# Attention and a routed expert layer on one core: weight, token and quarter sums moved from GpSimd to VectorE, slot lists by column ops, and new ranks

## The chip, the core and the metric

The kernel runs on one core of a Trainium2 chip. The core has TensorE (PE in the profile; PEld is its weight load), VectorE (DVE), ScalarE (ACT), GpSimd (POOL), SyncE (SP), which issues transfers, and 16 DMA engines. Each engine runs its own list of instructions in order and waits on semaphores for the others. The metric is the device time of one execution in microseconds; lower is better.

## The reference, cut to what matters

Eight sequences of 576 tokens with eight heads of 64 go through attention over a window of 128 tokens with a bias that grows with distance. The result, 4608 rows of 512, goes through a layer of eight experts of which each token takes two.

```python
scores = scale * q @ k.T + bias           # only 0 <= i - j < 128 counts
x = softmax(scores) @ v                   # heads side by side: [4608, 512]

noisy = x @ w_gate + log1p(exp(x @ w_noise)) * noise
top2 = two largest of noisy per token     # of 8 experts
top2_w = softmax over those two
for e in range(8):
    h = maximum(x[mask] @ w1[e], 0)       # 512 -> 1024
    out[mask] += top2_w * (h @ w2[e])     # 1024 -> 512
```

## The kernel before

**Order of the work.** The program is written as strands (Python generators). A strand yields an `Op` with an engine, a cost in microseconds and a rank, or an `Event`, or a ring of buffers. While the kernel is built, the class `Order` plays the strands through a simulated clock: each engine takes the waiting Op of least rank, and the instructions are emitted in that order. So every engine's list is fixed at build time by the costs and by the ranks, which come from constants at the top of the file (`LOAD`, `GATE`, `ROUTE`, `SCATTER`, `STAGE`, `LATE`, `SIZES` and so on). `either` offers an Op to ScalarE and VectorE, and `added` offers it to VectorE and GpSimd; whichever is free first by the simulated clock takes it, with one of the numbers of `LATE` as a handicap.

**Attention.** 32 head pairs are loaded, multiplied (`scores`), biased and reduced on VectorE (`top`, L540 and L548), exponentiated on ScalarE (`soft`, L564), transposed, masked on GpSimd (`split`, L597 and L598), and multiplied with the values (`weigh`). Rows go to DRAM (`xs`), and `gate` makes the logits of the experts.

**Routing.** For each sequence b, `route(b)` finds the two experts of each token (MAX8 at L852), gives each of the 2 x 5 choices per partition a slot number, and splits that into a line `ln` and a place `pl`. Then `which` (L891) compares all ten places with the numbers 0 to 63 in one instruction, and all ten lines with 0 to 79 in another, and `numbered` (L896) multiplies the first of these one-hots by the token numbers, on GpSimd or, in the last sequence, on VectorE. Ten products on TensorE (`list_`, L900) make the list of tokens by slot, which GpSimd adds into DRAM.

**Experts.** Expert 0 starts early in three blocks while the attention ends. The other seven have two blocks of 512 tokens (`wide`) and a smaller one each. All inputs are split into two half-precision parts (hi and lo), so a product takes three passes. A wide block's first layer works on halves: the 512 x 512 product of each pair of weight chunks is made from seven products of quarters (a scheme of Strassen's kind) and needs sums of quarters on three sides:

- weights, `summed_weights`: four subtractions of 128x256 in two parts (L1134) for each of 28 chunk pairs, then a cast `hi` and a residue `lo` (L1149);
- tokens, `turn_pair`: four adds or subtractions (L1337, L1338, L1340, L1341) for each of 28 pairs of token tiles, then a cast and residues (L1357), then a DMA transpose;
- products, `up_wide`: copies of the first two quarters (`copied`), their sum with two others in one op of 512 columns (`two_sums`, L1507), one more add of 256 columns behind it (L1510), sums with PSUM (`last_sum`, L1516), ReLU (L1546 on ScalarE, L1548 on VectorE) and residues (L1524, L1535). `two_sums` releases TensorE's next product, L1447.

`scaled_weight` casts the weights themselves (L279 on ScalarE or L281 on VectorE) and makes their residues (L1285). The second layer (L1578 for wide blocks, L1583 and L1571 for others) accumulates in PSUM; `result` scales by the gates and GpSimd adds the rows into the output by an indirect DMA (L1682). Gathers of token rows are L1295, also on GpSimd.

The sums are offered to both engines, in the token case as follows:

```python
    def added(a, b, rank, late, emit):
        return Op((("DVE", a, rank + max(late, 0.0)), ("POOL", b, rank + max(-late, 0.0))), lambda e: emit(engine[e]))
...
        for part in range(2):
            yield added(ADD * 2, ADDP * 2, rank, LATE[13], lambda g, part=part: sums_(g, part))
```

Of the kernel before, what the change touches and what calls it, by code (L numbers as in the profile page):

```python
# [8 lines left out]
F32 = mybir.dt.float32  # L9
F16 = mybir.dt.float16  # L10
BF16 = mybir.dt.bfloat16
I32 = mybir.dt.int32
U32 = mybir.dt.uint32
AF = mybir.ActivationFunctionType
OP = mybir.AluOpType
# [3 lines left out]
B, H, S, D = 8, 8, 576, 64  # L19
N, DM, E, F = B * S, H * D, 8, 1024  # L20
W = 128
NQ = 5
# [10 lines left out]
LINE, SPAN = 64, 10  # L33
# [6 lines left out]
WIDE, HALF = 512, 256  # L40
REST = CAP - 2 * WIDE
BLOCKS = tuple(((FROWS, c - FROWS),) if z < NF else ((0, WIDE), (WIDE, WIDE), (2 * WIDE, c - 2 * WIDE)) for z, c in enumerate(CAPS))
ZERO, EMPTY = -360.1, -14
LOAD = -70.1
VALUES = 211.5
GATE = (-6.6, 90.4, 356.8, 1.5)
ROUTE = (2.7, 19.6, 30.3, 85.8)
SCATTER = (192.6, -636.6, -1198.2, -775.2, -416.9)
FFN0, FFN1 = 160.9, 226.9
WEIGHTS = (150.4, 304.8)  # L50
TOKENS = 300.4
STAGE = (-13.0, 20.0, 8.1, -75.6, -10.3, 716.5, 87.3, 19.0)
MIDDLE = 77.8
RESULT = -175.8
SIZES = (35.1, -207.3, 1265.1)
SOON = -114.2
TIGHT = (1, 5, 7)
QUICK = (5, 7)
LATE = (-38.8, -263.4, 73.0, 226.7, -304.2, -361.8, -81.1, -258.9, 76.0, 16.9, -38.5, -10.3, -151.5, -115.4, 75.0)
LAG = 0.2  # L60
ADD, ADDP, TWS = 0.36, 0.9, 5
BEHIND = 2.7
TURN, MARGIN, LATE_BY = (0.3, 0.3), 1.0, 1.0
TURNED = 7e4
SLACK = 0.8
PACE, READ_BY, AHEAD = 0, 2.0, -28.3
HELD = 3
SWITCH, NEAR = 0.093, 3.6
TOP, SOFT, SPLIT = (1.27, 1.52, 0.92), (1.56, 1.56, 0.8), (0.85, 1.35, 0.85)
SP_COST = 0.45  # L70
DMA_RATE = 300e3
# [31 lines left out]
class Order:  # L103
# [15 lines left out]
    def spawn(self, strand):  # L119
        self.alive += 1  # L120
        self.at(self.now, lambda: self.advance(strand, None))
# [115 lines left out]
def attention_moe(ctx: ExitStack, tc: tile.TileContext, qk_, v, w_gate, w_noise, noise, w1, w2,  # L237
                  out, xs, slots, eye):
    nc = tc.nc
# [12 lines left out]
    spawn, put, mark = order.spawn, order.put, order.set  # L252
# [10 lines left out]
    def dve(us, rank, emit, join=True):  # L263
        return Op((("DVE", us, rank),), emit, join)
# [3 lines left out]

    def either(a, b, rank, late, emit):
        return Op((("ACT", a, rank), ("DVE", b, rank + late)), emit)  # L270

    engine = {"DVE": nc.vector, "POOL": nc.gpsimd}

    def added(a, b, rank, late, emit):
        return Op((("DVE", a, rank + max(late, 0.0)), ("POOL", b, rank + max(-late, 0.0))), lambda e: emit(engine[e]))

    def copy(e, o, i, **kw):
        if e == "ACT":
# [49 lines left out]
    steps_ = const.tile([128, E * SPAN], F16, name="steps")  # L328
# [489 lines left out]
    def route_tiles(z):  # L818
        return [ap_.tile(shape, dt, name=f"{name}{z}") for name, shape, dt in (
            ("y", [128, NQ, E], F32), ("u", [128, NQ, E], F32), ("l", [128, NQ, E], F32), ("tp", [128, NQ, 8], F32),  # L820
            ("idx", [128, NQ, 8], U32), ("ef", [128, NQ, 2], F32), ("oh", [128, NQ, 2, E], F32), ("both", [128, NQ, E], BF16),
            ("d", [128, NQ, 2], F32), ("gg", [128, NQ, 2], F32), ("rk", [128, NQ, E], F32), ("oh2", [128, NQ, 2, E], F32),
            ("ln", [128, NQ, 2], I32), ("pl", [128, NQ, 2], I32), ("gd", [128, NQ, E], F32), ("listed", [E * SPAN, LINE], F32),
            ("hot80", [128, 2 * NQ, E * SPAN], F16), ("hot64", [128, 2 * NQ, LINE], F16))]

    route_sets = [route_tiles(z) for z in range(2)]
# [2 lines left out]
    def route(b):  # L829
        yield gates[b]  # L830
        if b > 1:
            yield routed[b - 2]
        y_, u, l, tp, idx, ef, oh, both_, d, gg, rk, oh2, ln, pl, gd, listed, *hot = route_sets[b % 2]
        rank = 20 * b - ROUTE[kind(b)]
        V = nc.vector
        on, G, us = (dve, V, 0.75) if b == B - 1 else (pool, nc.gpsimd, 1.5)
        on_, N_ = (dve, V) if b in QUICK else (pool, nc.gpsimd)
        lg = lgs[b % 2]
        yield act(0.09, rank, lambda: nc.scalar.activation(u, lg[:, :, 8:16], AF.Abs))
# [45 lines left out]
        def lines_and_places():  # L885
            V.tensor_scalar(ln, pl, 6, None, op0=OP.arith_shift_right)
            V.tensor_scalar(pl, pl, LINE - 1, None, op0=OP.bitwise_and)

        def which(n_, of, hot_):
            shape = [128, 2 * NQ, n_]  # L890
            V.tensor_tensor(hot_, of.rearrange("p i k -> p (i k)")[:, :, None].to_broadcast(shape),  # L891
                            steps_[:, None, 0:n_].to_broadcast(shape), op=OP.is_equal)

        def numbered():
            t = hot[1].rearrange("p (i k) c -> p i (k c)", k=2)
            G.tensor_tensor(t, t, numbers[:, :, None].to_broadcast([128, NQ, 2 * LINE]), op=OP.mult)  # L896

        def list_(a):
            for z in range(2 * NQ):
# [60 lines left out]
        yield from chain(place, 0.3)  # L960

        mark(placed_)
        yield dve(0.75, rank, lambda: which(LINE, pl, hot[1]))
        spawn(number_them(on, us, rank, numbered, ready := Event()))
        yield dve(1.12, rank, lambda: which(E * SPAN, ln, hot[0]))
        yield ready
        a = yield (tb, rank)
        yield pe(0.4, rank, lambda: list_(a))
        yield dve(0.3, rank, lambda: whole_numbers(a))
# [16 lines left out]
    def first_ids(blk, cut, rank):  # L986
# [17 lines left out]
        blk.ix, blk.at = ix, cl  # L1004
        mark(blk.ids)
        spawn(weights_back(blk, rank))

    def number_them(on, us, rank, numbered, ready):
        yield on(us, rank, numbered)
        mark(ready)  # L1010

    def gates_out(b, rank, tp, d, oh, gg, gd, placed_):

# [111 lines left out]
    def summed_weights(e, a, rank, low, high):  # L1125

        (r0, there0, uses0), (r1, there1, uses1) = low, high
        done, (hi, lo) = sums[e, a]
        yield there0
        yield there1  # L1130
        s_ = yield (tsr, rank)

        def sums_(g, part):
            sub = lambda o, x, y: g.tensor_tensor(s_[:, 2 * o:2 * o + 2], x, y, op=OP.subtract)  # L1134
            if part == 0:
                sub(0, r1[:, 0:2], r0[:, 0:2])
                sub(2, r1[:, 2:4], r1[:, 0:2])
            else:
                sub(1, r1[:, 2:4], s_[:, 0:2])
                sub(3, r0[:, 2:4], s_[:, 2:4])  # L1140

        for part in range(2):
            yield added(ADD * 2, ADDP * 2, rank, LATE[12], lambda g, part=part: sums_(g, part))
        through_with(raw1, r0, uses0)
        through_with(raw1, r1, uses1)
        yield sized[e]
        sc = wsc[:, e, 0:1].bitcast(F32)
        yield either(1.04, 0.66, rank, LATE[5], lambda g: copy(g, hi, s_, scale=sc))
        yield dve(1.2, rank, lambda: nc.vector.scalar_tensor_tensor(lo, s_, sc, hi, op0=OP.mult, op1=OP.subtract))  # L1149
        put(tsr, s_)  # L1150
        yield order.now + SLACK
        mark(done)
# [162 lines left out]
    def turn_pair(blk, q, xp, rank):  # L1315
# [28 lines left out]
        nothing_ = hi[:, 0:4 * HALF].rearrange("p (a b) -> p a b", a=2)  # L1344
        yield act(1.12, rank, lambda: nc.scalar.activation(nothing_, rows, AF.Square, accum_out=big))
        for part in range(2):
            yield added(ADD * 2, ADDP * 2, rank, LATE[13], lambda g, part=part: sums_(g, part))
        yield dve(1.0, rank, powers)
        extra = xp[:, 2 * P:2 * P + 3 * HALF]
        parts_ = ((slice(0, 4 * HALF), rows, 4), (slice(4 * HALF, 7 * HALF), extra, 3))  # L1350
# [151 lines left out]
    def two_sums(c, y, rank, end, copies, done, u):  # L1502
        yield end
        for copy_ in copies:
            yield copy_
        both = c[:, 0:2].rearrange("p a b -> p (a b)")
        yield dve(0.6, rank - MIDDLE, lambda: nc.vector.tensor_tensor(both, y, both, op=OP.add))  # L1507
        yield order.now + SLACK
        mark(done)
        yield added(ADD, ADDP, rank - MIDDLE, LATE[14], lambda e: e.tensor_tensor(c[:, 4], c[:, 0], c[:, 1], op=OP.add))  # L1510
        mark(u)

    def last_sum(c, at, t, rank, end, ready_, done, whole):
# [478 lines left out]
```

## Time and profile before

| | |
|---|---|
| median of 3 runs | 1052.37 us (1047.01 to 1054.67) |
| profiled execution: time, span | 1055.15 us, 1053.4 us |
| busy, PE / DVE / ACT / POOL | 976.6 / 843.3 / 555.6 / 512.2 us |
| share of the span | 93% / 80% / 53% / 49% |
| mean granted clock of TensorE | 0.979 |

The span runs from the first to the last instruction. Busy time is the union of an engine's instructions. Matmuls are pipelined, so a busy TensorE is not one at its peak; in the attention stage its products are short. A wait is put down to the op that released it last.

### The profile page before, as it was taken

The page shows a single profiled execution, that of the slowest core. Times are in us where ns is not written, and L with a number is a line of the kernel's source. Part 1 is how long each engine was busy: PE and PEld are TensorE (multiplying, and loading weights), DVE is VectorE, ACT ScalarE, POOL GpSimd, SP SyncE. Part 2 cuts the span into 40 slices and gives each one's busy share as a digit, 9 for nine tenths or more (in the row PEclk, how much of TensorE's full clock was granted, in tenths as well). Part 3 has the DMA queues.
Part 4 walks back from the last instruction along what each step waited for, and adds up shares of the span by engine and source line. Part 5 has one row for each costly group of instructions (what it writes and reads, how often), then busy time and mean ns, then how long its engine had stood idle before and what let it go on. Part 6 is the DMA issues. An engine that isn't in the chain of part 4 may idle for free. (4 is left out here: it accounts for less than half of the span.)

```text
span 1053.4 us, 24584 instructions
## 1 busy us (share of the span) xinstructions
PE 976.6 (93%) x8656; PEld 669.9 (64%) x8656; DVE 843.3 (80%) x2639; ACT 555.6 (53%) x1484; POOL 512.2 (49%) x726
## 2 busy tenths in 40 slices
PE   8999998989998699979998999999899979998996
PEld 5766666655567466756676667666766666566663
DVE  8989999997668979696979898769978787879430
ACT  8988888832244445454543554445546354445221
POOL 3457677574444643633463437353726264553312
PEclk9999999989999999999999999999999989998998
DMA  9867897734699879777977679677979686776123
GB/s 324 310 212 251 271 344 236 274 68 108 139 221 203 193 214 161 173 156 205 134 155 171 178 144 181 171 205 167 143 220 194 167 194 157 143 166 114 29 29 49
DMA packets 236334, 188.84 MB, mean 179 GB/s; under 512 B 147056, under 2 KB 190352, under 8 KB 236208
## 3 DMA queue, kind: packets, MB, share of 16 engines
q1 hardware_dynamic: 218864, 148.31, 53.3%
q0 software_dynamic: 17344, 38.94, 20.2%
q8 instruction: 68, 1.11, 0.4%
q14 instruction: 58, 0.48, 0.1%
HBM read 116.24 MB, written 40.71 MB: 149 GB/s over the span
## 5 line engine op out<-in xcount | busy, mean ns | idle before, releaser
L1682 POOL DMA_INDIRECT out_dram<-yo,ix x69 | 114.6, 1662 | 72.4 <-ACT yo L279 30.0
L1578 PEld LDWEIGHTS <-hh 128*128 128x128 f16 x896 | 88.1, 99 | 84.3 <-issue 2.7
L1546 ACT ACTIVATE hh<-bank 128x256 f16<-128x256 f32 (+8 forms) x125 | 44.2, 356 | 142.7 <-PE bank L1421 82.0
L1447 PEld LDWEIGHTS <-wth 128*128 128x128 f16 x896 | 88.7, 99 | 37.9 <-issue 18.0
L1578 PE MATMUL bank<-w2ha,hl 128*128 128x512 f16 x288 | 110.1, 382 | 0.7 <-DVE hl L1535 0.7
L1578 PE MATMUL bank<-w2ha,hh 128*128 128x512 f16 x288 | 110.4, 383 | 0.0
L1578 PE MATMUL bank<-w2la,hh 128*128 128x512 f16 x288 | 110.2, 383 | 0.0
L1546 ACT ACTIVATE hh<-c 128x256 f16<-128x256 f32 (+1 forms) x98 | 50.2, 521 | 111.0 <-DVE c L1516 90.6
L564 ACT ACTIVATE p<-p,nm 128x128 f32<-128x128 f32 x256 | 99.3, 398 | 1.7 <-DVE nm L540 1.6
L1510 POOL TENSOR_TENSOR c<-c 128x256 f32<-128x256 f32 x32 | 32.3, 1010 | 125.6 <-DVE c L1507 106.7
L1578 PEld LDWEIGHTS <-hl 128*128 128x128 f16 x448 | 44.2, 99 | 55.0 <-issue 1.9
L279 ACT ACTIVATE c<-bank 128x256 f32<-128x256 f32 x92 | 34.3, 382 | 83.6 <-PE bank L1447 82.6
L1295 POOL DMA_INDIRECT xg<-xs_dram,ix x34 | 36.5, 1074 | 85.6 <-DVE ix L1042 55.3
L1447 PE MATMUL bank<-xhw,wth 128*128 128x256 f16 x224 | 62.9, 281 | 15.8 <-DVE c L1507 14.9
L1507 DVE TENSOR_TENSOR c<-bank,c 128x512 f32<-128x512 f32 x56 | 38.3, 684 | 47.0 <-PE bank L1447 46.4
L597 POOL TENSOR_SCALAR_AFFINE_SELECT pT<-pT 128x256 f32<-128x256 f32 (+1 forms) x80 | 45.5, 569 | 62.5 <-ACT pT L279 58.7
L540 DVE CUSTOM_DVE_ANT_0 p<-bank,bias 128x128 f32<-128x128 f32 x288 | 66.9, 283 | 0.9 <-ACT raw L1251 0.3
L1561 DVE SCALAR_TENSOR_TENSOR hl<-bank,hh 128x384 f16<-128x384 f32 (+8 forms) x88 | 31.1, 362 | 42.9 <-ACT hh L1546 38.5
L1447 PE MATMUL bank<-xhw,wtl 128*128 128x256 f16 x224 | 63.1, 281 | 0.8 <-DVE wtl L1149 0.8
L1447 PE MATMUL bank<-xlw,wth 128*128 128x256 f16 x224 | 63.1, 282 | 0.0
L1578 PE MATMUL bank<-w2hb,hh 128*128 128x512 f16 x160 | 61.1, 382 | 0.0
L1447 PE MATMUL bank<-xhe,wth 128*128 128x256 f16 x224 | 61.1, 273 | 0.0
(351 smaller groups left out, 3327.8 us busy)
## 6 DMA issues: line engine op xcount, KB each, us to landing
raw<-in_w_dram SPq DMA_DIRECT2D x144, 256.0 KB
mraw<-in_w_dram SPq DMA_DIRECT2D x56, 512.0 KB
qk<-in_qk_dram SPq DMA_DIRECT2D x32, 576.0 KB
vraw<-in_v_dram SPq DMA_DIRECT2D x16, 640.0 KB
out_dram<-xg SPq DMA_DIRECT2D x10, 1024.0 KB
xs_dram<-x SPq DMA_DIRECT2D x32, 256.0 KB
out_dram<-yo,ix POOLq DMA_INDIRECT x69
xs_dram<-x SPq DMA_DIRECT2D x8, 128.0 KB
```

The costliest lines, as they stand in the source:

```text
L279: nc.scalar.activation(o, i, AF.Copy, **kw)
L540: nc.vector.tensor_tensor_reduce(out=o, in0=i, in1=by, scale=-0.125, scalar=3.0e38, op0=OP.add, op1=OP.min, accum_out=m)
L564: nc.scalar.activation(pv, pv, AF.Exp, bias=nm[:, z, h:h + 1], scale=-1.0, accum_out=den[:, i, 2 * g + h:2 * g + h + 1])
L597: nc.gpsimd.affine_select(b, a, pattern, OP.is_ge, nothing, base=0, channel_multiplier=-1)
L1295: nc.gpsimd.indirect_dma_start(out=o, out_offset=None, in_=xs[0:blk.rows], in_offset=bass.IndirectOffsetOnAxis(ap=blk.at[0:r, j:j + 1], ax ...
L1447: nc.tensor.matmul(t, wp[:, at + kc], xp[:, 2 * o + kc], start=not add and kc + z == 0, stop=kc + z == 3, skip_group_check=add)
L1507: yield dve(0.6, rank - MIDDLE, lambda: nc.vector.tensor_tensor(both, y, both, op=OP.add))
L1510: yield added(ADD, ADDP, rank - MIDDLE, LATE[14], lambda e: e.tensor_tensor(c[:, 4], c[:, 0], c[:, 1], op=OP.add))
L1546: nc.scalar.activation(o, i, AF.Relu)
L1561: yield dve(0.07 + c * 0.00104, rank - MIDDLE, lambda: nc.vector.scalar_tensor_tensor(hl[:, 0:c], t[:, 0:c], 0.0, hh[:, 0:c], op0=OP.max, ...
L1578: nc.tensor.matmul(blk.y[j], h[:, cs], wp, start=a == 0 and z + m == 0, stop=a == 3 and z + m == 3)
L1682: ins = nc.gpsimd.indirect_dma_start(out=out, out_offset=bass.IndirectOffsetOnAxis(ap=blk.ix[0:r, j:j + 1], axis=0), in_=t[0:r], in_offset ...
```

## The change

All three kinds of sums are put on VectorE alone; `added`, the table of engines and the price of an add on GpSimd are gone, and the price of one on VectorE is 0.34 instead of 0.36. In the routing, line and place numbers are copied to floating point (`at`); instead of two wide compares and a multiplication there are twenty ops on VectorE, each of which makes one one-hot from a row of numbers and a scalar of its partition: ten of 64 columns that compare and multiply by the token number in the same op, and ten of 80 columns that compare. The strand that did the multiplication (`number_them`) is gone. All the constants that set ranks, handicaps and the lead of loads have other values.

```diff
-ZERO, EMPTY = -360.1, -14
-LOAD = -70.1
-VALUES = 211.5
-GATE = (-6.6, 90.4, 356.8, 1.5)
-ROUTE = (2.7, 19.6, 30.3, 85.8)
-SCATTER = (192.6, -636.6, -1198.2, -775.2, -416.9)
-FFN0, FFN1 = 160.9, 226.9
-WEIGHTS = (150.4, 304.8)
-TOKENS = 300.4
-STAGE = (-13.0, 20.0, 8.1, -75.6, -10.3, 716.5, 87.3, 19.0)
-MIDDLE = 77.8
-RESULT = -175.8
-SIZES = (35.1, -207.3, 1265.1)
-SOON = -114.2
+ZERO, EMPTY = -369.7, -14
+LOAD = -176.0
+VALUES = 264.2
+GATE = (28.7, 58.3, 273.1, -24.4)
+ROUTE = (-6.5, -64.7, 50.7, 56.9)
+SCATTER = (52.9, -732.8, -1277.6, -718.6, -208.6)
+FFN0, FFN1 = 159.2, 160.4
+WEIGHTS = (260.2, 307.4)
+TOKENS = 130.0
+STAGE = (128.3, 25.5, 7.9, -55.5, -24.4, 650.6, 199.2, 2.0)
+MIDDLE = 37.7
+RESULT = -108.3
+SIZES = (37.8, -49.2, 1152.7)
+SOON = -196.5
...
-LATE = (-38.8, -263.4, 73.0, 226.7, -304.2, -361.8, -81.1, -258.9, 76.0, 16.9, -38.5, -10.3, -151.5, -115.4, 75.0)
+LATE = (-36.7, -187.9, 194.5, 187.3, -443.9, -321.4, -78.2, -270.0, 39.8, 18.4, 65.3, -170.3, -195.9, -63.5, 40.7)
-ADD, ADDP, TWS = 0.36, 0.9, 5
-BEHIND = 2.7
+ADD, TWS = 0.34, 5
+BEHIND = 2.3
-PACE, READ_BY, AHEAD = 0, 2.0, -28.3
+PACE, READ_BY, AHEAD = 0, 2.0, 12.9
-SWITCH, NEAR = 0.093, 3.6
+SWITCH, NEAR = 0.093, 7.0
...
-            ("ln", [128, NQ, 2], I32), ("pl", [128, NQ, 2], I32), ("gd", [128, NQ, E], F32), ("listed", [E * SPAN, LINE], F32),
+            ("lp", [128, 2, NQ, 2], I32), ("at", [128, 2, NQ, 2], F32), ("gd", [128, NQ, E], F32), ("listed", [E * SPAN, LINE], F32),
...
             V.tensor_scalar(pl, pl, LINE - 1, None, op0=OP.bitwise_and)
-
-        def which(n_, of, hot_):
-            shape = [128, 2 * NQ, n_]
-            V.tensor_tensor(hot_, of.rearrange("p i k -> p (i k)")[:, :, None].to_broadcast(shape),
-                            steps_[:, None, 0:n_].to_broadcast(shape), op=OP.is_equal)
-
-        def numbered():
-            t = hot[1].rearrange("p (i k) c -> p i (k c)", k=2)
-            G.tensor_tensor(t, t, numbers[:, :, None].to_broadcast([128, NQ, 2 * LINE]), op=OP.mult)
+            V.tensor_copy(at, lp)
+
+        def places():
+            for z in range(2 * NQ):
+                i, k = z // 2, z % 2
+                V.tensor_scalar(hot[1][:, z], steps_[:, 0:LINE], at[:, 1, i, k:k + 1], numbers[:, i:i + 1],
+                                op0=OP.is_equal, op1=OP.mult)
+
+        def lines():
+            for z in range(2 * NQ):
+                V.tensor_scalar(hot[0][:, z], steps_[:, 0:E * SPAN], at[:, 0, z // 2, z % 2:z % 2 + 1], None, op0=OP.is_equal)
...
-        yield dve(0.75, rank, lambda: which(LINE, pl, hot[1]))
-        spawn(number_them(on, us, rank, numbered, ready := Event()))
-        yield dve(1.12, rank, lambda: which(E * SPAN, ln, hot[0]))
-        yield ready
+        yield dve(0.7, rank, places)
+        yield dve(0.7, rank, lines)
...
-            yield added(ADD * 2, ADDP * 2, rank, LATE[12], lambda g, part=part: sums_(g, part))
+            yield dve(ADD * 2, rank, lambda part=part: sums_(nc.vector, part))
...
-            yield added(ADD * 2, ADDP * 2, rank, LATE[13], lambda g, part=part: sums_(g, part))
+            yield dve(ADD * 2, rank, lambda part=part: sums_(nc.vector, part))
...
-        yield added(ADD, ADDP, rank - MIDDLE, LATE[14], lambda e: e.tensor_tensor(c[:, 4], c[:, 0], c[:, 1], op=OP.add))
+        yield dve(ADD, rank - MIDDLE, lambda: nc.vector.tensor_tensor(c[:, 4], c[:, 0], c[:, 1], op=OP.add))
```

## Rows read from the trace of the kernel before

**Rows 1.** Table of stages: stretch and length, busy us of PE, PEld, DVE, ACT, POOL, PEclk, DMA, GB/s.
```profile
0.00:240.00 240.00, 220.12 (x2895) 151.09 (x2896) 222.79 (x1152) 192.01 (x778) 147.80 (x318) 0.98 0.75 251
340.00:1000.00 660.00, 617.45 (x4720) 429.72 (x4720) 537.01 (x1211) 317.64 (x610) 307.02 (x334) 0.98 0.76 166
```

**Rows 2.** Waits of TensorE, 340 to 1000 us: total us, times, longest us.
```profile
PE bank L1447 <- DVE c L1507: 14.9, 6, 5.2
PE bank L1583 <- DVE hl L1561: 6.4, 7, 2.1
...
PE bank L1663 <- DVE yt L283: 0.2, 1, 0.2
```

**Rows 3.** Sums on GpSimd: stages of L1134 (DVE, POOL busy); groups by line, 240:1053.4.
```profile
340.00:1000.00 660.00, 16.03 (x34) 67.96 (x74) 0.98 0.76 166
...
L1510 POOL TENSOR_TENSOR c<-c 128x256 f32<-128x256 f32 x32 | 32.3, 1010 | 125.6 <-DVE c L1507 106.7 <-DVE wex L506 10.5 <-DVE diag L493 5.0
...
L1337 POOL TENSOR_TENSOR xp<-xp 128x256 f32<-128x256 f32 x8 | 10.8, 1346 | 3.2 <-ACT hh L1546 2.8 <-ACT w2ha L279 0.4
...
L1337 POOL TENSOR_TENSOR xg<-xg 128x256 f32<-128x256 f32 x4 | 4.2, 1046 | 0.1
```

**Rows 4.** Single lines: ns at minimum, median and maximum, first and last start, shapes.
```profile
L1516 DVE TENSOR_TENSOR c<-bank,c x112: 401/414/426, 350.0 to 1025.0; 128x256 f32<-128x256 f32 x112
...
L1285 DVE SCALAR_TENSOR_TENSOR w2lb<-raw,wsc,w2hb x20: 733/742/1207, 334.1 to 972.5; 128x512 f16<-128x512 f32 x20
...
L1535 DVE SCALAR_TENSOR_TENSOR hl<-c,hh x56: 672/682/1218, 352.9 to 1025.3; 128x512 f16<-128x512 f32 x56
...
L1524 DVE SCALAR_TENSOR_TENSOR hl<-c,hh x56: 406/418/1180, 351.8 to 1025.9; 128x256 f16<-128x256 f32 x56
...
L281 DVE TENSOR_SCALAR w1ha<-raw,wsc x14: 474/480/943, 81.6 to 955.2; 128x512 f16<-128x512 f32 x14
...
L1357 DVE SCALAR_TENSOR_TENSOR th<-xp,fit,th x28: 996/1274/1856, 324.4 to 968.5; 128x1024 f16<-128x1024 f32 x14, 128x768 f16<-128x768 f32 x14
...
L1510 POOL TENSOR_TENSOR c<-c x32: 717/728/1721, 348.7 to 1022.6; 128x256 f32<-128x256 f32 x32
L1510 DVE TENSOR_TENSOR c<-c x24: 406/416/978, 384.0 to 1003.9; 128x256 f32<-128x256 f32 x24
```

**Rows 5.** Groups of VectorE by line and shape, 240:1053.4: busy us, mean ns, idle before.
```profile
L1535 DVE SCALAR_TENSOR_TENSOR hl<-c,hh 128x512 f16<-128x512 f32 x56 | 42.2, 753 | 1.3 <-ACT hh L1546 1.0
...
L1341 DVE TENSOR_TENSOR xp<-xp 128x256 f32<-128x256 f32 x7 | 3.8, 540 | 0.2
```

**Rows 6.** Timelines of VectorE, GpSimd and TensorE ahead of 865 us: start us, us.
```profile
858.88 1.21 DVE L1285 SCALAR_TENSOR_TENSOR w2lb<-raw,wsc,w2hb 128x512 f16<-128x512 f32 x1
860.01 1.22 DVE L1535 SCALAR_TENSOR_TENSOR hl<-c,hh 128x512 f16<-128x512 f32 x1
861.15 0.94 DVE L1524 SCALAR_TENSOR_TENSOR hl<-c,hh 128x256 f16<-128x256 f32 x1
862.02 0.94 DVE L281 TENSOR_SCALAR w1ha<-raw,wsc 128x512 f16<-128x512 f32 x1
862.89 1.47 DVE L1357 SCALAR_TENSOR_TENSOR th<-xp,fit,th 128x768 f16<-128x768 f32 x1
...
858.75 0.80 POOL L1134 TENSOR_TENSOR ts<-raw,ts 128x256 f32<-128x256 f32 x1
...
862.76 0.78 POOL L1341 TENSOR_TENSOR xg<-xg 128x256 f32<-128x256 f32 x1
...
865.01 0.37 PE L1447 MATMUL bank<-xhw,wth 128*128 128x256 f16 x1 [3.34 <-DVE c L1507]
```

**Rows 7.** One-hots: L891 over the span (DVE busy); L896; MAX8 (busy us, mean ns).
```profile
sum 1053.40, DVE 17.37; mean DVE 8.68
...
L896 POOL TENSOR_TENSOR hot<-hot,numbers x7: 1257/1260/2081, 89.7 to 258.0; 128x640 f16<-128x640 f16 x7
...
L852 DVE MAX8 tp<-l 128x8 f32<-128x8 f32 x40 | 3.5, 153 | 3.0 <-POOL l L919 2.9
```

More of the change, by code (lines that the diff above doesn't have):

```diff
@@ L270, in either @@
         return Op((("ACT", a, rank), ("DVE", b, rank + late)), emit)
-    engine = {"DVE": nc.vector, "POOL": nc.gpsimd}
-    def added(a, b, rank, late, emit):
-        return Op((("DVE", a, rank + max(late, 0.0)), ("POOL", b, rank + max(-late, 0.0))), lambda e: emit(engine[e]))
     def copy(e, o, i, **kw):
@@ L832, in route @@
             yield routed[b - 2]
-        y_, u, l, tp, idx, ef, oh, both_, d, gg, rk, oh2, ln, pl, gd, listed, *hot = route_sets[b % 2]
+        y_, u, l, tp, idx, ef, oh, both_, d, gg, rk, oh2, lp, at, gd, listed, *hot = route_sets[b % 2]
+        ln, pl = lp[:, 0], lp[:, 1]
         rank = 20 * b - ROUTE[kind(b)]
         V = nc.vector
-        on, G, us = (dve, V, 0.75) if b == B - 1 else (pool, nc.gpsimd, 1.5)
         on_, N_ = (dve, V) if b in QUICK else (pool, nc.gpsimd)
@@ L1006, in first_ids @@
         spawn(weights_back(blk, rank))
-    def number_them(on, us, rank, numbered, ready):
-        yield on(us, rank, numbered)
-        mark(ready)
     def gates_out(b, rank, tp, d, oh, gg, gd, placed_):
```

## The prediction

> **What bounds the kernel now.** I read the table of stages first [rows 1]. The run falls into an attention stage (to 240 us), a short first wave of experts, and the long second wave, 340 to 1000 us. In the attention stage VectorE is busy for 222.8 of 240 us and TensorE's 220 us are made of short products with waits between them, so VectorE sets its pace. In the second wave TensorE is busy for 617.45 of 660 us at a granted clock of 0.98, that is, nearly always at the higher level of 2.4 GHz. TensorE is the bound there, and all that another engine can give back is the 42.6 us in which it idles. The waits of TensorE in that stage come next [rows 2]: thirteen of the sixteen groups name VectorE, from 14.9 us on the two-sum op of L1507 down to 0.2 us, 39.8 us in all. So the question of this case is whether VectorE reaches the sums and residues that TensorE waits for sooner or later than now.
>
> VectorE is busy for 537 of the 660 us, 81%, so it isn't full. It is late in bursts. The third view is the timeline ahead of one such burst [rows 6]: TensorE waits 3.34 us before 865.01 us for L1507, and in the six microseconds ahead of it VectorE ran five ops, each near half a microsecond longer than usual. Undisturbed they last 742, 682, 418, 480 and 996 ns (medians; the last the minimum, as its row mixes two widths) [rows 4]; here they took 1.21, 1.22, 0.94, 0.94 and 1.47 us, which is 0.47 + 0.54 + 0.52 + 0.46 + 0.47 = 2.46 us more. In the same stretch GpSimd ran five adds, the first at 858.75 and the last at 862.76 us [rows 6]. The minimum, median and maximum of the lines [rows 4] tell the same: the op that reads one PSUM and one SBUF operand (L1516) spans 401 to 426 ns over 112 executions, while those on SBUF operands alone lie near their medians most of the time and reach 0.94 to 1.86 us. GpSimd's own add has 717 ns as minimum and 1721 as maximum. On this chip, an add on GpSimd and an op of VectorE on SBUF operands delay each other. In sums, the mean less the median, times the count, over the 26 groups of VectorE that can be hit in this way (from 56 x (753 - 682) ns = 4.0 us on L1535 to 7 x (540 - 424) ns = 0.8 us on L1341) [rows 4, 5] is about 43 us. Beside each of the five lengthened ops of the burst an add was running, so I put the 43 us to the adds.
>
> **The change, part by part.** *Sums moved from GpSimd to VectorE.* These are 74 weight sums (68.0 us of GpSimd), 32 quarter sums (32.3 us) and 48 token sums, twelve for each of four lines in eight groups (10.8 us for the largest) [rows 3]. That is 154 adds of 128x256. On VectorE one takes 416 ns (L1510) [rows 4], or some 350 ns where the next op starts before its end, an estimate from the MAX8 row, in which each op lasts 153 ns but forty take 3.5 us, 88 ns apiece [rows 7]. So VectorE gains 154 x 0.35 to 154 x 0.42 = 54 to 64 us of work, and loses the 43 us of lengthening: net +11 to +21 us on 537 of 660, from 81 to about 84%. VectorE doesn't become the bound on average. In throughput the trade is nearly even. What can pay is *where* the time lies. The lengthening falls on whatever op VectorE happens to run, the ones that TensorE waits for included. A sum on VectorE stands where its rank puts it, and VectorE has over 120 us of idle time in that stage.
>
> I price this on the stall at 865.01 us [rows 6]. If all five adds go to a place where TensorE isn't waiting, 2.46 of its 3.34 us go, 74%. If all five stay in the same run, 2.46 less 5 x 0.42 = 2.1 leaves 0.36 us, 11%. The middle, 42%, of the 39.8 us behind VectorE [rows 2] is 17 us; the ends are 4 and 29 us. I take the middle, because part of the sums has slack (weights are summed ahead of their block) and part has none: the quarter sum of L1510 stands between L1507 and the last residue of the same step, and the token sums stand between a gather and its turning. For those the shorter latency helps a little, 416 ns against a mean of 1010 [rows 3, 4], but TensorE's waits name other ops, so I count nothing for it.
>
> *GpSimd freed.* About 150 us less work there lets scatters and gathers be issued earlier. No large wait of TensorE names GpSimd [rows 2], so zero; if a gather was late without being named, the gain is inside the 3 us of waits that don't name VectorE.
>
> *One-hots by columns.* Gone per route: two compares on VectorE, 17.37 us for eight routes or 2.2 us each, and GpSimd's multiplication of 1.26 us median, 2.08 at most (in the last route that one was on VectorE already) [rows 7]. New: a copy of 20 numbers and 20 ops on 64 or 80 columns. No row shows such an op. From below it is the 88 ns spacing of MAX8 on 8 columns, from above the 153 ns that a lone one lasts [rows 7]; with 0.15 us for the copy this gives 1.9 to 3.2 us a route, -0.3 to +1.0, or -2 to +8 us over eight routes. I take 88 ns, as the twenty ops don't depend on each other, and so about nothing. The multiplication that vanishes had also lengthened some VectorE ops beside it, which supports the lower end. VectorE is 93% busy in the attention stage [rows 1], so whatever it is counts nearly in full, and the upper end stays for the range.
>
> *Ranks set anew.* Every engine runs its list in the order fixed at build time, and all the constants behind that order differ. The profile can't price this. It bounds the gain: TensorE's idle in the second wave is 42.6 us, and VectorE's in the attention stage 17 us [rows 1]. No row gives a lower bound on the loss; I allow 8 us in either direction and count zero for the forecast.
>
> Sum: -17 us. The profiled execution has a span of 1053.4 and a time of 1055.15 us, 1.75 us around the span; that becomes a span near 1036 and a time near 1038. Its time lies 2.8 us above the median of the three runs, 1052.37, so the forecast is 1052.37 - 17 = **1035.5 us**. Runs of before spread from 1047.01 to 1054.67 us, 0.7%; about 1% is what a measurement can tell from no change.
>
> **The rivals.**
>
> *Nearly all of the stalls behind VectorE go.* At 74% or more of 39.8 us, with a few microseconds from a better order: -29 to -35 us, 1020 us. For it: every one of the larger waits is behind VectorE [rows 2], and its excess disappears altogether. Against: the adds must run somewhere, and three quarters of relief needs all of them out of the way.
>
> *VectorE pays back what it wins.* The adds stay in the bursts, relief is 4 us or less, and the one-hots or the order eat that: 1050 us, between 1044 and 1058. For it: the throughput sum is +11 to +21 us against it, and bursts are exactly where sums become due. Against: 120 us of idle time to place them in.
>
> *Slower: sums in front of the two-sum.* VectorE takes its list in order. A sum of two adds (0.8 us) that stands ahead of L1507 in a step delays it, and behind it queue the residues of the same step; the next products on TensorE wait for them. There are 56 such steps (L1535 has one execution per step) [rows 5]. With one in three hit and nothing hidden, 19 x 0.8 = 15 us, 1067 us. It decides once VectorE idles clearly less ahead of L1507 than now and TensorE's wait for L1507 grows beyond 14.9 us. Against: the planner prices a sum on VectorE as VectorE time, while lengthening was nowhere in its prices.
>
> *Slower: columns at full length.* The spacing of MAX8, 88 ns for an op that lasts 153 [rows 7], says that independent small ops overlap. If a column op holds VectorE for its whole duration instead, and its 64 to 80 columns lengthen it to 0.2 us (an estimate between 153 ns at 8 columns and 418 ns at 256) [rows 4, 7], a route costs 4.15 us against 2.2: +2 us, 16 us over eight routes in a stage that VectorE paces, 1052 + 16 - 4 = 1064 us with little relief. The Trainium skill, "VectorE: DVE Perf Modes", section "The DRAIN you can't avoid", speaks for this one: it says that the next op does not start until the pipe has emptied, and its "Rules for kernel authors" advise fewer ops. The trace disagrees as to MAX8, in the spacing just named.
>
> **How the numbers follow.** Half relief, as forecast: 0.50, mostly faster than 1041.8 us. Nearly full relief: 0.13. Paid back: 0.25. Sums in front: 0.07. Columns: 0.05. Faster by over 1%: nearly all of the first and all of the second, 0.60. Within 1%: the rest of the first and most of the third, 0.28. Slower: the last two, 0.12. The range takes both ends of the relief (29 and 4 us), the 8 us of order on either side and the paid-back case, which reaches 1058: 1017 to 1058 us; the slower two and the extreme of full relief lie outside, under 2 in 10.
>
> **What would show it.** In the changed profile no tensor-tensor add of 128x256 of these lines is left on GpSimd, and the maxima of L1535, L1285, L1357 and the second group of L1524 come down from about 1.2 us to their medians, 0.7 us on the narrow ones: that is the lock-step of the two engines gone. VectorE's busy time in the second wave stays within 545 to 560 us. TensorE's idle in it is near 25 instead of 42.6 us, and its wait for L1507 below 10. The attention stage's VectorE time differs by less than 8 us, with the column ops about 0.1 us apart. I am wrong in the mechanism if the maxima stay, in the placing if they fall and TensorE's waits for VectorE don't, in the one-hots if the attention stage ends over 5 us later, and by the unpriced order if time moves in a stage where neither the sums nor the one-hots lie.

## The result and the profile after

The changed kernel takes 1038.42 us (median of 4 runs, 1035.63 to 1039.77), 0.988 of the kernel before, with a 95% interval of 0.983 to 0.992 (four runs of the kernel before beside it have a median of 1053.52 us). The forecast was 1035.5 us. The sum came out near, but two of its terms were far off, in opposite directions, as the rows show.

First the table of stages of the changed kernel, at the bounds used before (busy us of PE, PEld, DVE, ACT, POOL, then PEclk, DMA share, GB/s):

```profile
0.00:240.00 240.00, 209.86 (x2788) 146.18 (x2789) 223.18 (x1246) 184.56 (x753) 127.00 (x302) 0.95 0.72 241
340.00:1000.00 660.00, 641.37 (x5028) 451.75 (x5027) 556.19 (x1401) 335.91 (x641) 191.89 (x197) 1.00 0.80 172
```

Against [rows 1], TensorE idles for 18.6 instead of 42.6 us in the second of these stretches, and GpSimd is busy for 115 us less. In the first, TensorE has less done by 240 us: 209.86 against 220.12 us. So the same bounds don't hold the same work. A cut at each kernel's own first product of a wide block (342.2 us before, 361.7 after) does. The two stretches of the kernel before, then those of the changed one:

```profile
0.00:342.20 342.20, 317.63 (x3622) 213.86 (x3623) 297.27 (x1410) 227.14 (x847) 193.26 (x379) 0.99 0.78 228
342.20:1053.40 711.20, 658.95 (x5037) 456.03 (x5034) 546.03 (x1230) 328.48 (x638) 318.98 (x347) 0.98 0.72 156
```

```profile
0.00:361.70 361.70, 324.61 (x3611) 219.13 (x3612) 316.58 (x1576) 229.11 (x845) 173.01 (x368) 0.96 0.73 219
361.70:1037.50 675.80, 648.33 (x5048) 451.53 (x5045) 542.23 (x1368) 333.58 (x641) 191.16 (x197) 1.00 0.76 162
```

TensorE's idle time in the second wave (length less PE busy) fell from 52.3 to 27.5 us, 24.8 less. Ahead of it the idle time rose from 24.6 to 37.1 us, 12.5 more. TensorE's busy time fell by 10.6 us in the wave, where the granted clock is 1.00 instead of 0.98, and rose by 7.0 us ahead of it, where the clock is 0.96 instead of 0.99: 3.6 us less in all. That is -24.8 + 12.5 - 3.6 = -15.9 us, the whole difference of the spans. VectorE's busy time in the wave didn't rise: 542 against 546 us, though it runs 138 ops more there. Ahead of the wave it rose by 19 us.

TensorE's waits from 340 to 1000 us in the changed kernel (total us, times, longest us; L1498 is the former L1507, L1515 the former L1524), which answer to [rows 2]:

```profile
PE bank L1438 <- DVE c L1498: 6.1, 9, 1.4
PE bank L1438 <- DVE hl L1515: 3.1, 5, 1.0
```

With nine smaller groups of at most 1.0 us each, the waits that name VectorE sum to 14.7 us, from 39.8. No single one exceeds 1.4 us; before, the longest was 5.2. The lines of [rows 4], now L1526 (former L1535), L1515 and L1501 (former L1510), with minimum, median and maximum in ns:

```profile
L1526 DVE SCALAR_TENSOR_TENSOR hl<-c,hh x56: 671/682/743, 371.3 to 1010.1; 128x512 f16<-128x512 f32 x56
...
L1515 DVE SCALAR_TENSOR_TENSOR hl<-c,hh x56: 404/418/426, 373.1 to 1010.7; 128x256 f16<-128x256 f32 x56
...
L1501 DVE TENSOR_TENSOR c<-c x56: 403/416/475, 369.6 to 1007.9; 128x256 f32<-128x256 f32 x56
```

The medians are the same to the nanosecond and the maxima of 1.2 us are gone. What went wrong stands in the lines of the one-hots, the ten compares with two scalars (L888) and the ten with one (L893), with their busy time over the whole span, and timelines of the routes at 182 and 225 us (start, us):

```profile
L888 DVE TENSOR_SCALAR hot<-steps,at,numbers x80: 282/294/684, 84.5 to 282.0; 128x64 f16<-128x64 f16 x80
...
sum 1037.50, DVE 19.52; mean DVE 9.76
...
L893 DVE TENSOR_SCALAR hot<-steps,at x80: 144/238/640, 87.9 to 284.0; 128x80 f16<-128x80 f16 x80
...
sum 1037.50, DVE 13.52; mean DVE 6.76
...
182.44 2.14 DVE L888 TENSOR_SCALAR hot<-steps,at,numbers 128x64 f16<-128x64 f16 x10
...
225.63 3.07 DVE L888 TENSOR_SCALAR hot<-steps,at,numbers 128x64 f16<-128x64 f16 x10
...
229.90 1.58 DVE L893 TENSOR_SCALAR hot<-steps,at 128x80 f16<-128x80 f16 x10
```

At 225 us ten places take 3.07 us and ten lines 1.58; at 182 us, where GpSimd stands idle, ten places take 2.14. Over the whole span the two lines take 19.52 and 13.52 us of VectorE, 4.1 us a route, where I had put 1.8.

### The profile page after: what moved, and what is told of

It reads as the page before. It is cut to its first block, busy times and chain, and to the rows that moved or that the text cites. A ratio compares the mean times of both kernels' runs of the same rounds, so it can differ in the third digit from the quotient of the medians.

```text
span 1037.5 us, 24610 instructions
## 1 busy us (share of the span) xinstructions
PE 972.9 (94%) x8656; PEld 670.7 (65%) x8656; DVE 858.8 (83%) x2943; ACT 562.7 (54%) x1485; POOL 364.2 (35%) x565
## 3 DMA queue, kind: packets, MB, share of 16 engines
q1 hardware_dynamic: 218864, 148.31, 54.4%
## 5 line engine op out<-in xcount | busy, mean ns | idle before, releaser
L1673 POOL DMA_INDIRECT out_dram<-yo,ix x69 | 118.6, 1719 | 178.3 <-ACT yo L274 100.7
L1286 POOL DMA_INDIRECT xp<-xs_dram,ix x35 | 41.1, 1175 | 255.6 <-DVE ix L1033 174.1
L1537 ACT ACTIVATE hh<-c 128x512 f16<-128x512 f32 (+1 forms) x103 | 52.5, 523 | 116.8 <-DVE c L1507 114.5
L1537 ACT ACTIVATE hh<-bank 128x256 f16<-128x256 f32 (+8 forms) x117 | 41.2, 353 | 116.1 <-PE bank L1412 61.2
L1286 POOL DMA_INDIRECT xg<-xs_dram,ix x34 | 39.0, 1147 | 75.9 <-DVE ix L1033 42.3
L1498 DVE TENSOR_TENSOR c<-bank,c 128x512 f32<-128x512 f32 x56 | 38.3, 685 | 32.3 <-PE bank L1438 31.8
L514 PE MATMUL bank<-qk 64*64 64x192 f32 (+1 forms) x1024 | 55.6, 332 | 9.3 <-DVE raw L355 4.7
L592 POOL TENSOR_SCALAR_AFFINE_SELECT pT<-pT 128x256 f32<-128x256 f32 (+1 forms) x80 | 42.0, 525 | 58.8 <-ACT pT L274 51.0
L1242 ACT ACTIVATE mraw<-mraw 128x1024 f32<-128x1024 f32 x56 | 58.6, 1046 | 6.8 <-DMA mraw<-in_w_dram 6.8
L1438 PE MATMUL bank<-xhw,wtl 128*128 128x256 f16 x224 | 61.0, 273 | 0.8 <-DVE fit L494 0.8
```

What stands on the lines that cost most here:

```text
L514: nc.tensor.matmul(s[h][a:a + 64, o + first_:o + first_ + c_], qk[half, i * 128 + a:i * 128 + a + 64], qk[half, QW + k0 + first_:QW + k0 + ...
L592: nc.gpsimd.affine_select(b, a, pattern, OP.is_ge, nothing, base=0, channel_multiplier=-1)
L1242: yield act(us, rank, lambda: nc.scalar.activation(v, v, sum_, accum_out=o))
L1286: nc.gpsimd.indirect_dma_start(out=o, out_offset=None, in_=xs[0:blk.rows], in_offset=bass.IndirectOffsetOnAxis(ap=blk.at[0:r, j:j + 1], ax ...
L1438: nc.tensor.matmul(t, wp[:, at + kc], xp[:, 2 * o + kc], start=not add and kc + z == 0, stop=kc + z == 3, skip_group_check=add)
L1537: nc.scalar.activation(o, i, AF.Relu)
```

## The experiments

All comparisons are with the kernel before, run on the same chip; the runs are spread over several chips, so two of them are best compared by their ratios. "Idle" is TensorE's, ahead of the first wide product and from there on, and "VectorE" its busy time in that second stretch, all from the profiled execution.

| kernel | median us | ratio (95%) | first wide product | idle ahead | idle in wave | VectorE in wave |
|---|---|---|---|---|---|---|
| before | 1052.37 | 1 | 342.2 | 24.6 | 52.3 | 546 |
| changed | 1038.42 | 0.988 (0.983, 0.992) | 361.7 | 37.1 | 27.5 | 542 |
| e1 new operations, old ranks | 1075.88 | 1.022 (1.018, 1.026) | 376.1 | 48.5 | 42.1 | 549 |
| e2 old operations, new ranks | 1058.98 | 1.006 (1.003, 1.008) | 347.3 | 28.4 | 53.5 | 548 |
| e3 sums alone, old ranks | 1057.28 | 1.003 (1.001, 1.006) | 337.7 | 21.1 | 54.4 | 548 |
| e4 columns alone, old ranks | 1099.41 | 1.045 (1.041, 1.049) | 375.8 | 49.0 | 58.0 | 544 |
| e5 sums, new ranks, wide one-hots | 1047.46 | 0.994 (0.992, 0.996) | 354.4 | 33.6 | 39.8 | 544 |
| e6 the same, mixed ranks | 1039.79 | 0.987 (0.982, 0.991) | 354.1 | 32.5 | 33.8 | 544 |
| e7 changed, dummy adds on GpSimd | 1082.37 | 1.029 (1.026, 1.032) | 365.3 | 37.7 | 56.4 | 592 |
| e8 changed, dummy fills on GpSimd | 1043.42 | 0.992 (0.989, 0.995) | 361.0 | 35.0 | 28.6 | 544 |
| e9 changed, wide one-hots in the same order | 1020.45 | 0.971 (0.969, 0.974) | 347.6 | 28.2 | 26.0 | 542 |
| e10 changed, price of an add 0.36 | 1037.25 | 0.990 (0.985, 0.994) | 359.6 | 34.0 | 26.1 | 540 |
| e11 before, adds swapped in place | 1049.29 | 0.998 (0.994, 1.001) | 344.6 | 25.1 | 50.7 | 550 |
| e12 as e9, multiplication on GpSimd | 1021.51 | 0.971 (0.967, 0.975) | 345.0 | 29.1 | 27.7 | 541 |

**Operations against ranks.** The first four take the change apart: its constants (e1, e2), its sums (e3) and its columns (e4, from the kernel before).

```diff
 e1: changed kernel, ZERO ... NEAR as in the kernel before
 e2: kernel before, ZERO ... NEAR as in the changed kernel, ADD, ADDP = 0.36, 0.9
 e3: kernel before
-            yield added(ADD * 2, ADDP * 2, rank, LATE[12], lambda g, part=part: sums_(g, part))
+            yield dve(ADD * 2, rank, lambda part=part: sums_(nc.vector, part))
...                                                # the token sums and the quarter sum likewise
 e4: kernel before, with places(), lines(), lp and at of the changed one
```

> The changed kernel with every constant of before. Theory A (the sums on VectorE end the mutual delay with GpSimd and shorten the second wave by some 30 us, the column ops cost some 16 us of VectorE in the attention stage, the new order is worth little): 1032 to 1045 us. Rival B (the new ranks bring the gain and the operations hardly matter): within 1% of before, 1043 to 1062, or slower. In both, no op of VectorE on SBUF operands is lengthened in the second wave; under A the second wave (first to last product of the wide blocks, 682.4 us before and 647.8 after) is near 650, under B near 680.

> The kernel before with every constant of the changed one (and the old prices of an add, 0.36 on VectorE and 0.9 on GpSimd). Theory A: the mutual delay stays, the second wave stays at 675 to 690 us, 1045 to 1075 us in all. Rival B: the gain is in the constants, so near 1038 us, second wave near 650.

> The kernel before, its constants kept, with the three kinds of sums on VectorE alone; the compares stay wide and their multiplication on GpSimd. Theory A: the whole relief without the cost of the columns: 1015 to 1032 us, the attention stage as before (last biased row reduction near 216 us), the second wave near 650 us. Rival B: within 1% of before.

> The kernel before, its constants kept, with the one-hots by twenty column ops and the sums offered to both engines as before. Theory A: VectorE gains some 16 us of one-hots, nearly all of it ahead of the experts, so 1060 to 1070 us with the last biased row reduction 8 to 14 us later than 216. Rival (the column ops are hidden): within 1% of before.

Neither theory stood. The new operations under the old ranks are 2% slower, the old operations under the new ranks half a per cent slower, and both together are faster. Rival B falls with e2: the ranks alone bring nothing. Theory A falls with e3: the sums alone bring nothing either. The mutual delay is gone in e3 (L1535 has a maximum of 752 ns), yet TensorE idles for 54.4 us in the wave. e4 came out far above what either theory allowed. I had to form a third: that taking the adds off GpSimd is an even trade for VectorE, whose time is 540 to 550 us in every one of these kernels, and pays only in an order in which the adds stand apart from what TensorE waits for. One pair speaks against "only": e1 is e4 with the sums on VectorE, under the same old ranks, and is 2.2% faster (1075.88 against 1099.41 us). Beside the columns the sums pay without new ranks; why is open.

**The even trade, with the order held.** e11 leaves the plan of the kernel before as it is and issues on VectorE, in the same place, what the plan gave to GpSimd.

```diff
-    engine = {"DVE": nc.vector, "POOL": nc.gpsimd}
+    engine = {"DVE": nc.vector, "POOL": nc.vector}
```

> The kernel before with its plan untouched, but each add that the plan gives to GpSimd is issued on VectorE, at the point where it stood. The order on TensorE and ScalarE is that of before. By the throughput sum of the prediction (43 us of lengthening less, 54 to 64 us of adds more, all in the bursts) 1048 to 1062 us. Rival (the mutual delay alone was the loss): 1020 to 1040 us.

It came out as the throughput sum says, 0.998 of before. The row of its wave and that of the residue line:

```profile
344.60:1052.30 707.70, 656.98 (x5036) 455.44 (x5034) 550.03 (x1380) 328.67 (x638) 182.58 (x197) 0.98 0.73 156
...
L1535 DVE SCALAR_TENSOR_TENSOR hl<-c,hh x56: 669/681/748, 355.5 to 1025.0; 128x512 f16<-128x512 f32 x56
```

150 more ops on VectorE (1380 against 1230), 136 us less on GpSimd, hardly an op lengthened in the wave, and VectorE's busy time is 550 against 546 us. TensorE's idle time is 50.7 against 52.3.

**The mutual delay, with the order held.** e7 and e8 keep the changed kernel's order on TensorE, VectorE and ScalarE, instruction by instruction, and give GpSimd something to do beside each of the 168 places where a strand makes sums: an add that reads SBUF, or two fills that only write. Nobody reads what they write.

```diff
+    def beside():                                  # e7
+        two = ident[:, None, :].to_broadcast([128, 2, 128])
+        nc.gpsimd.tensor_tensor(spare_[:, 1600:1856].rearrange("p (a b) -> p a b", a=2), two, two, op=OP.add)
+    def beside():                                  # e8
+        nc.gpsimd.memset(spare_[:, 1600:2048], 0.0)
+        nc.gpsimd.memset(spare_[:, 1600:1856], 0.0)
```

> The changed kernel with an extra add of 128x256 on GpSimd beside each of the 168 sum instructions groups on VectorE, between constants and a scratch area that nobody reads; the order on every other engine is that of the changed kernel. Theory A (adds on GpSimd and ops of VectorE on SBUF operands delay each other): L1526's residue of 512 columns goes from 684 to about 740 ns mean with maxima of 1.2 us, VectorE gains 30 to 55 us of busy time in the wave, TensorE idles 10 to 25 us more, 1048 to 1065 us. Rival (the gain is from shorter latency of the sums and the order alone): under 5 us more, through later gathers and scatters at most.

> As the last, but in place of each add two fills of 448 and 256 columns, about as long in sum, that read nothing. If the mutual delay needs GpSimd to read SBUF: residues with two SBUF operands stay at their medians, and the time is within 6 us of the changed kernel, 1036 to 1044 us, the rest being later gathers. If any long op on GpSimd delays VectorE: as with the adds, 1048 us or more. Casts on VectorE from SBUF to SBUF may be delayed in either case.

The wave of e7 and its residue line (L1532 here), then those of e8:

```profile
365.30:1080.00 714.70, 658.34 (x5049) 455.54 (x5046) 592.25 (x1368) 333.25 (x641) 312.44 (x354) 0.98 0.72 154
...
L1532 DVE SCALAR_TENSOR_TENSOR hl<-c,hh x56: 672/682/1101, 375.8 to 1052.4; 128x512 f16<-128x512 f32 x56
```

```profile
361.00:1039.80 678.80, 650.23 (x5048) 453.44 (x5045) 543.54 (x1368) 333.48 (x641) 316.00 (x511) 0.99 0.76 162
...
L1532 DVE SCALAR_TENSOR_TENSOR hl<-c,hh x56: 673/682/748, 370.6 to 1011.8; 128x512 f16<-128x512 f32 x56
```

GpSimd is busy for 312 and 316 us, nearly the same. With the adds, VectorE's 1368 ops take 50 us longer and the kernel takes 44 us more than the changed one, above the range that theory A had; in the wave TensorE idles 28.9 us more, and its busy time is 10.0 us longer at a granted clock of 0.98 instead of 1.00. With the fills, VectorE takes 1 us and the kernel 5 us more. So it is not GpSimd's time that costs, nor later gathers behind it (5 us at most), but that it reads SBUF while VectorE works on SBUF operands. The 56.4 us of idle time in e7 don't show what the new order is worth by itself, as VectorE carries the sums and the delay at once there; e2, with its adds on GpSimd, is the run for that.

**Other mixtures of order and operations.** e5 and e6 put the wide compares back and let the planner make a new order.

```diff
 e5: e3 with the constants of the changed kernel
 e6: e5 with ZERO, LOAD, VALUES, GATE, ROUTE, SCATTER, FFN0, FFN1, WEIGHTS, TOKENS, STAGE,
     LATE[2], LATE[3], LATE[9] and SIZES[0] of the kernel before
```

> The changed kernel with its constants and its sums on VectorE, but the one-hots as before: two wide compares and the multiplication on GpSimd. Theory A (sums and order together gave the second wave 35 us; the column ops take 15 us of VectorE, 33.0 against 18.1 us, and more of the attention stage): the start of the wide blocks falls from 361.7 us to 340 to 348, the wave stays at 675 to 690 us, 1018 to 1032 us in all. Rival B (the constants fit exactly these operations, and any other set of operations loses the order's worth): 1045 to 1065 us with a wave over 695 us.

> As the last, but with the constants of before for loads, attention, gates, routes and the first wave (ZERO to TOKENS, STAGE, three of LATE, the first of SIZES), and the new ones for the second wave. Theory A: start of the wide blocks as before, 337 to 345 us, wave 675 to 690, 1015 to 1032 us. Rival B: wave over 695 us, 1040 us or more.

Neither theory fits: e5 is 0.6% faster than before, a time in the range of rival B with a wave of 693.0 us, just short of what B asked; e6 equals the changed kernel, between the two ranges. Their wide blocks start at 354 us, later than theory A had in either. Both keep part of the wave's gain (39.8 and 33.8 us of idle) and neither all of it, so the constants alone, without the plan that they made with the columns, don't give it. How much a small disturbance costs was asked of e10, which alters nothing but the price of an add.

```diff
-ADD, TWS = 0.34, 5
+ADD, TWS = 0.36, 5
```

> The changed kernel with nothing but the planner's price of an add set from 0.34 back to 0.36, so the same instructions in another order with the same ranks. If the ranks express where the sums belong, the time stays within 5 us, 1033 to 1044. Rival (the constants fit this one order by chance, and any disturbance loses it): 1045 us or more.

1037.25 us, one of four runs at 1045.03: the time holds within some 2 per mille (0.990 against 0.988), and the wave's idle is 26.1 us. A disturbance as small as this one doesn't lose the gain; the larger ones of e5 and e6 lose part of it.

**The columns, with the order held.** e9 keeps the plan and exchanges what is inside the two operations.

```diff
         def places():
-            for z in range(2 * NQ):
-                i, k = z // 2, z % 2
-                V.tensor_scalar(hot[1][:, z], steps_[:, 0:LINE], at[:, 1, i, k:k + 1], numbers[:, i:i + 1],
-                                op0=OP.is_equal, op1=OP.mult)
+            which(LINE, pl, hot[1])
+            t = hot[1].rearrange("p (i k) c -> p i (k c)", k=2)
+            V.tensor_tensor(t, t, numbers[:, :, None].to_broadcast([128, NQ, 2 * LINE]), op=OP.mult)
 
         def lines():
-            for z in range(2 * NQ):
-                V.tensor_scalar(hot[0][:, z], steps_[:, 0:E * SPAN], at[:, 0, z // 2, z % 2:z % 2 + 1], None, op0=OP.is_equal)
+            which(E * SPAN, ln, hot[0])
```

> The changed kernel with its order on every engine kept, but inside the two operations of the one-hots the wide compares and the multiplication of before, all on VectorE, in place of the twenty column ops and their copy. Theory A (the column ops cost 33.0 us of VectorE plus 1.5 for the copies, the wide form on VectorE about 8 x 2.8 = 22 us, and the attention stage is paced by VectorE): one-hots 20 to 23 us, wide blocks start 5 to 11 us earlier than 361.7, 1028 to 1034 us. Rival (the attention stage waits for something else): within 3 us of 1038.

1020.45 us, 0.971 of before: better than expected, and better than both kernels. The stretches of e9, and the busy time over the span of its compares (L886) and of its multiplications (L892):

```profile
0.00:347.60 347.60, 319.41 (x3610) 215.11 (x3611) 302.77 (x1432) 228.16 (x845) 178.70 (x368) 0.97 0.78 226
347.60:1021.80 674.20, 648.22 (x5049) 451.63 (x5046) 541.91 (x1368) 333.47 (x641) 190.22 (x197) 0.99 0.78 163
...
sum 1021.80, DVE 14.98; mean DVE 7.49
...
sum 1021.80, DVE 6.69; mean DVE 3.35
```

VectorE is busy for 13.8 us less ahead of the wave (302.77 against 316.58), the wave starts 14.1 us earlier, and it is as short as that of the changed kernel (674.2 against 675.8 us).

Last, the multiplication went back to GpSimd in that order, as a second test of the even trade.

```diff
-            V.tensor_tensor(t, t, numbers[:, :, None].to_broadcast([128, NQ, 2 * LINE]), op=OP.mult)
+            nc.gpsimd.tensor_tensor(t, t, numbers[:, :, None].to_broadcast([128, NQ, 2 * LINE]), op=OP.mult)
```

> As the run with the wide one-hots in the changed kernel's order, but the multiplication of each route on GpSimd. VectorE saves 8 x 0.83 = 6.6 us, GpSimd gains 8 x 1.26 = 10 us, which read SBUF and so delay neighbours on VectorE, and the list's products wait for GpSimd, which stands behind the masks of the attention. Theory A (an even trade, as with the sums): 1017 to 1024 us. Rival (VectorE's share is all that counts in the attention stage): 1012 to 1016 us.

1021.51 us, 0.971 of before with an interval of 0.967 to 0.975: even.

This run also shows what the order is worth once the sums are on VectorE. e12 and e3 do practically the same operations (sums on VectorE, wide compares, multiplication on GpSimd, but for the last route of e3) and differ in the order: 0.971 against 1.003, some 34 us, with 27.7 against 54.4 us of idle time in the wave.

## Why the prediction was right, and which terms were not

**What binds.** Right as to the engines: TensorE sets the pace of the second wave, and what it lost there it lost to VectorE. But its 42.6 us of idle time were not all that could be given back. The wave is 35.4 us shorter, 24.8 us by idle time and 10.6 us by TensorE's busy time at a granted clock of 1.00 instead of 0.98. Ahead of the wave the same goes the other way: 12.5 us of idle time and 7.0 us of busy time, at 0.96 instead of 0.99. The prediction had no term for the clock.

**The mutual delay.** The mechanism is shown by e7 and e8, in which the other three engines run the same instructions in the same order and GpSimd is busy for as long. Its size was read about rightly: 43 us of lengthening by rows, and 50 us more VectorE time in e7 for 168 dummy adds.

**The even trade of throughput.** I put it at +11 to +21 us for VectorE; e11 shows +4. Counted op by op, the ops that last over 1.2 times their median carry 47 us of lengthening in the wave of the kernel before, so by e11 the 150 adds cost some 51 us there, 0.34 us each, the lower of my two prices. The conclusion that the gain can't come from throughput was right, and e3 and e11 show the "paid back" rival to be the outcome under the old ranks and in the old order. That it comes from the place of the adds was not shown. From the first wide product to 1000 us, counted over the stretches of 0.1 us and more in which TensorE idles, VectorE spends 7.6 of 46.2 us on adds in e11 and 2.4 of 19.7 us in the changed kernel: the other ops left those stretches as well. What is shown (e12 against e3) is the worth of the order as a whole.

**Relief of the stalls.** Mis-sized. From the stall at 865 us I had 11% if the adds stay and 74% if they go, and took 42%. In the old order it is near nothing (e11 and e3, with 41.2 and 41.1 us of waits behind VectorE from 340 to 1000 us). In the new one these waits fall from 39.8 to 14.7 us, 63%, and TensorE's idle by 24.8 us over the wave instead of 17.

**Ranks set anew, counted zero.** This is where the rest lies. The ranks alone give +0.6% (e2), so as a term of its own, zero was not far off. But with the sums on VectorE the order makes nothing into 27 us: 54.4 us of idle in e3, 27.7 in e12. The new constants alone give about half of that, 14.6 us, without the columns (e3 to e5) as with them (e1 to the changed kernel); the rest came with the plan that the columns and their prices made. The sum treated placing and ranks as separate terms, and they are one. Which of the constants does it was not settled; e6, with those of the second wave alone, has 33.8 us of idle there.

**One-hots by columns, counted as nothing.** The largest error, and the step that failed is the price of an op. I took 88 ns from the spacing of MAX8. By busy time they cost 169 ns with one scalar (13.52 us for 80) and 244 ns with two (19.52 us for 80): 33.0 us in eight routes against 21.7 in e9 and 18.2 before (17.37 and the last route's 0.82). e9 against the changed kernel shows what that is in time, with the order held: 1038.42 less 1020.45, or by ratios 0.988 against 0.971, some 17 us. In a plan made anew the wide compares don't bring it back: e5, with 0.994, is slower than the changed kernel.

The rival "columns at full length" had 16 us and was given a chance of 0.05. Its price came true, but not its mechanism. The ops do overlap: 244 ns apiece is less than the 282 ns that the shortest of them lasts, and at 182 us ten of some 294 ns take 2.14 us. What was wrong was to take over the spacing of an op of 8 columns that lasts 153 ns for ops of 64 and 80 columns that last 294 and 238 ns at the median. The rule in the Trainium skill, "VectorE: DVE Perf Modes", section "The DRAIN you can't avoid", that the next op waits until the pipe has emptied, does not fit these rows, and fits MAX8 no better; the same section adds that a next op that is not held starts earlier. That the 3.07 us at 225 us come from GpSimd's masks beside the ops is likely and was not tested.

The sign named for this error showed: the last row reduction of the attention starts at 239.8 us, against 215.8 before. In e9 it starts at 228.1, so the columns are about half of that delay, and the rest came with the new order.

With that, the measured change of some -14 us is the sum of about -31 us (sums with an order that suits them, as e9 has it) and +17 us (columns), where I had -17 and 0. It came out right in sum only, by luck: two errors nearly cancelled.

**Slower in front of the two-sum.** It did not happen: TensorE's wait for that op is 6.1 us, from 14.9.

**Left open.** The columns cost 45 us in e4, where the adds are still offered to GpSimd. With the sums on VectorE they cost some 19 us under the same old ranks (e1 against e3), close to the 17 us in the new order (e9 against the changed kernel). So the old ranks alone don't make them dear; columns and adds on GpSimd together do. Three quarters of the 45 us are ahead of the wave, which starts 33.6 us later, with 49.0 us of idle time instead of 24.6; TensorE's busy time rises too, by 13.7 us over the span, at a mean granted clock of 0.965 instead of 0.979. The plan prices ten columns at 0.7 us and they take 1.7 to 2.4, so the order is built on wrong times; that this is the cause was not shown.

## What to carry to other kernels

Two engines that delay each other share their time: moving work from one to the other can leave the busy time of the engine that takes it where it was. What it earned here depended on the order (1.003 in e3, 0.971 in e12 with practically the same operations), so operation and order have to be tried together, and each also with the order held, to see which one paid. When a change bundles several edits, cost each by the row of an operation of the same form (operand kinds, scalars), not by any small op; a near-zero term with a wide upper end deserves its own experiment. A swap inside an operation, with the plan untouched, separates the price of an instruction from the price of a new order at once, and here it gave the best version.

## What the runs showed of the hardware that I had not expected

An add of 128x256 on GpSimd and fills of 448 and 256 columns hold GpSimd for about as long, but only the add delays VectorE's residues, which have two SBUF operands: maximum 1101 against 748 ns. Casts on VectorE from SBUF to SBUF, with one tensor operand, seem to be delayed by the fills as well, which I had only allowed for: in e8 the seven of 128x1024 tokens average 861 against 751 ns in the changed kernel, by three long ones. The first group below is of e8, the second of the changed kernel (busy us, mean ns, idle before):

```profile
L276 DVE TENSOR_SCALAR th<-xg,fit 128x1024 f16<-128x1024 f32 x7 | 6.0, 861 | 0.0
```

```profile
L276 DVE TENSOR_SCALAR th<-xg,fit 128x1024 f16<-128x1024 f32 x7 | 5.3, 751 | 0.0
```

The Trainium skill, "SBUF — State Buffer", section "SBUF: two separate sides", says both: VectorE and GpSimd hold a shared pair of ports for a whole instruction, and an op with two SBUF inputs meets it only against a GpSimd op that reads SBUF, while one in a two-port mode meets it against any. The rows agree as to which ops are lengthened; the ports themselves no run here shows.

The narrower of the two column ops is the longer one: the compare of 64 columns that also multiplies by a second scalar lasts 294 ns at the median and at least 282, the one of 80 columns without it 238 and 144. Whether the second scalar or the multiplication costs this was not separated.
